# Giving every product of an attention and MLP kernel more than 64 rows of the array

## The chip, the cores and the metric

The kernel runs on one core of a Trainium2 chip. The metric is device time in microseconds, the median of several executions. The engines are TensorE (PE, whose weight loads are listed apart as PEld), VectorE (DVE), ScalarE (ACT) and GpSimd (POOL); the queue of SyncE (SP) issues every DMA. They run beside each other and wait for each other by semaphores; each works through its own list strictly in the order in which it was written.

## The reference

Four sequences of 576 positions pass through three blocks, in float32:

```python
# attention, per batch (4) and head (8), head_dim 64; cum is a running sum of max(s, 0)
scores = where(causal, -1e9, q @ k.T / 8 + minimum(-(cum[:, None] - cum[None, :]), 0))
x = softmax(scores) @ v                      # heads side by side: 576 x 512 per batch
# MLP: tokens, then channels
u = x + (relu(x.T @ w_tok1) @ w_tok2).T      # 576 -> 256 -> 576
y = u + relu(u @ w_ch1) @ w_ch2              # 512 -> 1536 -> 512
# gated output
gate = sigmoid(causal 5-tap convolution of y with conv_w)
out = (gate * (y @ w_val)) @ w_out
```

## The kernel before

Most products are done in float16 with each operand split into an upper and a lower half ("hi" and "lo"), so one float32 product becomes three: hi x hi, hi x lo and lo x hi, added up in PSUM.

**Stages.** A pair is two heads of one batch; there are 16 pairs. The queries of a head are cut into five tiles, `QT`: the first 64 positions, then four tiles of 128. Per pair the kernel loads q, k and v, scales them by a power of two found from their largest magnitude (`scales`, which asks `over_partitions` for a maximum across partitions: a transpose by PE, then a product with 3 rows), splits them, and turns q and k by a transposing DMA (`turn_qk`). Per tile `score` computes the scores, `expo` the exponentials, `p_split` cuts these into halves and turns them by a transposing DMA into `pT`, and `av` multiplies them by v (`v16`) into the PSUM bank `xbank`. Then `norm`, `x_value`, `x_split` and `x_turn` produce the pair's columns of x, and `tok1` and `tok2` the token MLP. Batch 0 is done "wide": its probabilities stay float32 and are turned by PE (`p_turn`) rather than by DMA. When all four pairs of a batch are done, its channel MLP and gated output run (`ch1`, `ch2`, `val`, `outp`; tiles `c`, `v`, `o`), and the next batch's attention is interleaved with them. The weights are decoded, summed (`ws`), scaled (`wf`) and split while batch 0 is under way.

**Rows of the array.** A product uses as many rows of the array as it sums over. In `av` the keys of a tile are cut from position 0 into blocks of 128, so the last block of each tile has 64 keys:

```python
K = TAIL if m == i else P              # TAIL is 64, P is 128
for pl, vl in ((0, 0), (0, 1), (1, 0)):
    PE.matmul(o, lhsT=self.pT[i, hh][:K, pl * (i + 1) + m, 0:M], rhs=self.v16[:K, vl, hh, m, :], ...)
```

`tok1` sums over the five tiles of positions, of which the first has 64 rows; `x_turn` transposes the first tile with 64 rows; the product of `over_partitions` has 1 or 3 rows, that of a weight's `scale` 1, and the transposes of the convolution's taps 5.

**What sets the order.** `ORDER` (from line 79) is a written list of steps, each an engine's letter and a task's number (P is PE, A ACT, V DVE, G POOL, S SP). `Plan.run` (line 422) goes through it and lets that task do its next step on that engine. A planner beside it keeps an assumed time for each engine, from costs in `cost_pe`, `cost_dma` and the like. Those times decide one thing in the program: where PE is assumed to wait, `keep_warm` (line 302) fills part of the gap with warming products of a zero tile (`idle`), whose result nobody reads.

Of the kernel before, what the change touches and what calls it, by code (L numbers as in the profile page):

```python
# [8 lines left out]
F32 = mybir.dt.float32  # L9
# [10 lines left out]
TINY = 2.0 ** -90  # L20
# [28 lines left out]
    u16=2, hT=7, mA=3, mB=2,  # L49
# [30 lines left out]
S0 V0 S5 P6 A7 A7 V7 P7 V7 S136 S8 A9 P1 S137 V1 V1 S136 S10 P1 V1 V1 A1 A9 V1 G137 S188 G188 V9 A1 V1 S1 A11 A11 P9  # L80
V9 S16 S19 P17 S25 S138 A2 A2 V2 A139 S28 V11 P11 V11 V12 P12 V12 V12 A18 A139 A139 P139 V139 V139 A18 V18 P139 V139
G3 A13 A20 A20 V139 V139 A140 V20 V13 A14 A141 V140 P18 V14 A15 V141 S142 S30 S142 S187 V18 V15 P20 V20 P26 A27 A27
V27 A29 V21 A29 V29 P27 P29 V27 P21 V21 A143 P158 P168 V21 V22 V22 A23 G23 A31 A31 P146 V29 P144 V144 A145 S32 V168
A169 V146 A147 P175 P172 S187 P152 V152 A153 P150 V150 S189 A33 P156 P148 A148 P166 A151 V172 P173 V156 V173 V31 P31
P154 A33 V33 V166 V31 A190 A154 A190 P154 V158 A167 A154 A190 S39 P40 A41 A41 P33 V33 V34 V175 P34 V34 V34 P170 A159
A157 A170 P190 V190 P176 V176 A177 V35 V190 P154 A154 P149 P149 P160 A160 V41 P170 P190 V190 V190 P160 P155 A174 S42
S44 S46 V35 P41 P155 A160 P160 V190 V191 V194 V191 A192 V192 S193 P178 A160 P161 P161 V162 A41 G41 A170 P170 A178
P178 A36 G36 A170 V162 V162 A178 P178 V162 V163 A164 V164 P171 P171 V37 V37 G38 V38 G4 G4 P165 A178 P179 P179 V180
A47 S53 S238 A45 A43 A43 V43 A47 V47 V180 A45 V45 S193 P226 P207 V226 P201 V207 P197 V201 P195 P227 P217 P209 A165
A181 A182 V182 P183 A183 V217 A218 S240 P184 P223 V197 A198 V24 V195 A196 P199 V209 A202 S239 G239 A208 P184 V223  # L90
P224 V224 S238 A241 P45 A184 V184 P43 V43 P203 V203 A199 P200 P200 A241 V227 P219 P185 A241 P241 A225 A204 A210 V241
V45 S56 P47 A47 P185 V241 P205 A205 P241 V185 V186 P211 A211 V241 V186 P54 A57 V241 P205 A205 V219 P211 A57 S58 S60
S67 V241 P205 A211 P211 A205 P206 P206 G47 V48 A228 S291 V57 P57 A211 P212 V245 V57 A242 V242 A243 V243 S244 S244
A220 A55 P212 V213 P48 V48 P229 V186 V213 P221 A229 P229 A221 G4 A55 V48 P221 V213 V213 V214 A229 V55 A221 P229 G49
P221 V49 P216 A221 A61 P68 A69 P55 P222 P222 A229 P230 V50 A69 V55 V215 V50 A59 V215 V69 P230 V231 A61 P246 V246
S289 P258 P254 A59 A247 S290 P69 V231 S289 V258 A259 P252 V252 A253 P274 V274 A216 P248 P260 P277 V248 A249 P250
A232 V254 A255 G51 G51 G52 V277 V260 A250 P275 V275 P278 P256 G233 P270 G290 A261 P262 A256 V69 S70 A276 A292 V270
A271 V61 P268 V278 P256 V268 A256 V59 S463 G463 P251 P251 A292 P256 A256 A292 A269 P61 V61 S72 A262 P59 V59 S74 P292
V292 P257 P272 A272 P262 A262 P272 V52 V292 P292 P262 A71 A272 A71 P257 V62 P62 A279 V292 V292 P272 V233 P235 P235
V292 A294 V71 V296 V294 P280 P71 A293 V293 S295 A235 V235 V62 V71 S76 A280 V62 P234 S295 A262 P263 P263 A73 A73 V73  # L100
V264 V264 V264 A272 A63 V63 P280 A75 A75 S462 P73 V73 S78 V64 A280 A234 S462 P236 P236 V236 V75 V264 P280 A280 P75
A77 A77 V265 P267 P273 A266 A267 V237 A75 S80 G75 V64 P305 P299 V77 P309 P325 A65 V266 P297 V297 A298 G65 G66 P77
A77 P273 V305 A306 V237 P321 V299 A300 A79 A79 V321 P319 V319 P281 P328 A320 V309 A310 V237 V325 P303 A465 A465 P311
# [12 lines left out]
S110 S112 A111 S114 V527 A97 V97 G98 V98 S501 A111 A523 V111 P111 P351 A348 V348 A346 V346 S577 G527 G99 A113 A113
P351 P353 P353 V99 A374 V523 S525 V111 A115 V375 A115 A350 V350 A352 V352 P369 A376 P355 P355 G100 V115 P115 G577
V100 P357 V507 A354 V354 A101 V101 V102 S121 P122 V102 P357 A526 V113 P113 S525 P528 P359 P359 P369 V105 V341 V528
P361 P361 S576 A115 S124 G115 A356 V356 P530 A123 S576 V103 V103 V113 S126 V375 V492 A508 A510 G510 S510 A123 A360
A125 A358 A125 V360 P363 P363 V116 P116 V123 P123 A579 A104 A579 V125 P125 V116 P365 P365 V530 P535 A531 V104 A579  # L120
V116 V358 P370 P367 P367 S578 A362 V376 V535 P553 V362 P544 A117 V492 V492 V117 A529 A532 G532 A364 A123 S128 V492
V493 P502 S532 P502 A366 G123 V364 P579 V366 V544 G118 V118 A127 P537 V537 P560 P511 P511 P398 P398 P370 A494 A368
V368 P542 A533 G533 S533 P371 A536 A539 G539 S539 A119 P371 A129 V125 A545 A127 V119 A120 A129 V579 A538 V127 P127
V579 P579 A547 V494 V129 P129 V120 V542 P373 P373 A543 V579 P555 P377 P377 V372 P495 V127 V579 G547 V579 A580 A540
G540 V553 A554 P563 G557 A581 V512 V512 V513 P534 A514 P534 V555 A556 P378 P378 V560 P561 A495 P380 P380 V580 S547
A583 V581 V557 V129 V130 P130 V561 P381 P381 V584 S540 P541 P541 V130 A546 V546 V514 P515 P516 A562 V130 S582 V379
V563 P564 V564 P516 S557 A566 V566 A558 A515 S582 P592 P587 V587 P585 P400 A516 A565 P594 V594 S546 P548 P548 P382
# [148 lines left out]
class Plan:  # L276
# [40 lines left out]
    def cost_pe(self, name, a, k):  # L317
        if name == "transpose":
            ns = max(cols(a[1]), a[1].shape[0]) / 2.4 * 2
        else:  # L320
            n = cols(k["rhs"])
            ns = max(40.0, n / 2.4 + 2.5) if k["rhs"].dtype != F32 else max(n, cols(k["lhsT"])) / 2.4 * 4
# [1359 lines left out]
```

## Time and profile before

| | |
|---|---|
| median of 3 runs | 734.91 us (733.26 to 738.43) |
| profiled execution | 735.01 us, of which the span of the instructions is 733.0 us |
| mean granted clock of TensorE | 0.974 of full speed |
| busy time | PE 695.4 us, DVE 517.3, ACT 397.9, POOL 178.6 |

Busy time is the time in which at least one instruction of the engine runs. A matmul's record also holds the time that it spends in the array after the next one has started, so PE can look busy while its products follow each other at a longer distance than they need to. What a product costs in a full queue is read from starts: the time from one group's first start to the next group's.

### The profile page before, as it was taken

The numbers are of one execution on the slowest core, as the hardware profiler recorded it, in microseconds if no ns is written. First come the engines' busy times: TensorE is split into PE (matmuls) and PEld (weight loads), VectorE is DVE, ScalarE is ACT, GpSimd is POOL, SyncE is SP. The second block draws the span as 40 slices with busy tenths as digits, with TensorE's granted clock in tenths as the row PEclk, the third lists the DMA queues.
The fourth block names the chain that finished last, engine by engine and source line by source line (L and its number), as shares of the span: only waits on it lengthen the run. The fifth ranks groups of instructions, "written<-read, shape, count | busy, mean of one in ns | idle before, by whom it ended". The sixth has DMA issues, their size and how long they took to land.

```text
span 733.0 us, 16461 instructions
## 1 busy us (share of the span) xinstructions
PE 695.4 (95%) x6340; PEld 522.4 (71%) x6340; DVE 517.3 (71%) x1508; ACT 397.9 (54%) x834; POOL 178.6 (24%) x264
## 2 busy tenths in 40 slices
PE   3899999998999999999999899999999999999997
PEld 3677877766677777676777677676777777668864
DVE  5777797658997887777688786598478852344663
ACT  4687787747775775545544563456556512213233
POOL 0112304122224334251232032332222312000410
PEclk9999999869999999999999999999999999999999
DMA  8645564736739576754646446382927320000001
GB/s 242 161 147 155 145 186 148 173 83 151 185 68 167 80 140 132 113 102 89 127 94 105 102 97 106 52 168 42 176 43 124 87 37 1 30 1 9 1 30 64
DMA packets 197911, 76.35 MB, mean 104 GB/s; under 512 B 188389, under 2 KB 188485, under 8 KB 197834
## 3 DMA queue, kind: packets, MB, share of 16 engines
q1 hardware_dynamic: 197834, 75.32, 48.0%
q8 instruction: 49, 0.80, 0.5%
q14 instruction: 28, 0.23, 0.1%
HBM read 33.50 MB, written 4.83 MB: 52 GB/s over the span
## 4 chain that ended last, share of the span: by engine, by line
PE 46%; DMA 5%; DVE 2%; SPq 2%; ACT 1%; POOL 1%; issue 1%; ACTq 0%; POOLq 0%; DVEq 0%
PE c L258 24%; PE o L258 6%; PE v L258 5%; PE xbank L258 4%; PE t L258 3%; DMA qkT<-qk 3%; PE S L258 3%; SPq L258 2%; DMA qk<-qkT 1%; PE xm L258 1%; DMA pT<-p 1%; PE xT L258 1%; DVE x L258 1%; ACT qk L258 0%; DMA stg<-in_k_dram 0%
## 5 line engine op out<-in xcount | busy, mean ns | idle before, releaser
L258 PEld LDWEIGHTS <-arena 128*128 128x128 f16 (+1 forms) x3168 | 287.1, 99 | 81.8 <-issue 6.5
L258 PE MATMUL c<-hT,arena 128*128 128x256 f16 (+1 forms) x1152 | 162.0, 288 | 0.0
L258 PE MATMUL c<-u,arena 128*128 128x256 f16 (+1 forms) x1152 | 159.9, 288 | 0.2 <-DVE hT L258 0.2
L258 ACT ACTIVATE x<-x,st 128x576 f32<-128x576 f32 (+4 forms) x160 | 86.7, 556 | 70.8 <-DVE st L258 69.8
L258 DVE CUSTOM_DVE_ANT_0 x<-S,mask,sc 64x64 f32<-64x64 f32 (+4 forms) x160 | 74.7, 482 | 44.6 <-PE S L258 41.0
L258 POOL TENSOR_TENSOR p<-x,p 64x64 f16<-64x64 f32 (+4 forms) x71 | 58.4, 824 | 155.6 <-ACT p L258 71.1
L258 PE MATMUL xbank<-v,pT 128*128 128x65 f16 (+3 forms) x1240 | 86.1, 209 | 1.5 <-DMA pT<-p 1.0
L258 ACT ACTIVATE hT<-c 128x320 f16<-128x320 f32 (+1 forms) x96 | 37.2, 403 | 87.7 <-PE c L258 87.7
L258 PE MATMUL S<-qk 67*64 67x64 f16 (+4 forms) x192 | 53.7, 290 | 12.2 <-DMA qk<-qkT 12.1
L258 DVE SCALAR_TENSOR_TENSOR hT<-c,hT 128x320 f16<-128x320 f32 (+1 forms) x96 | 41.2, 448 | 30.1 <-ACT hT L258 30.0
L258 DVE SCALAR_TENSOR_TENSOR gate<-R,cwt,gate 128x320 f32<-128x320 f32 (+1 forms) x116 | 60.5, 534 | 1.0
L258 PEld LDWEIGHTS <-pT 128*128 128x128 f16 (+2 forms) x1080 | 48.2, 98 | 14.9 <-issue 2.9
L258 PE MATMUL o<-arena,g 128*128 128x512 f16 (+1 forms) x240 | 57.2, 380 | 0.0
L258 PE MATMUL S<-qkT 128*64 128x64 f16 (+4 forms) x192 | 54.2, 293 | 0.0
L258 PE MATMUL v<-x,arena 128*128 128x256 f16 (+1 forms) x384 | 53.6, 286 | 0.0
L522 PE MATMUL xbank<-idle 128*128 128x112 f16 x573 | 47.1, 235 | 2.6 <-DVE x L258 1.9
L522 PEld LDWEIGHTS <-idle 128*128 128x128 f16 x573 | 38.6, 111 | 6.5 <-issue 3.2
L258 ACT ACTIVATE p<-x 128x576 f16<-128x576 f32 (+4 forms) x69 | 31.9, 464 | 16.6 <-DMA pT<-p 10.4
L258 PEld LDWEIGHTS <-g 128*128 128x128 f16 (+1 forms) x240 | 22.7, 100 | 23.5 <-issue 2.1
L258 PE MATMUL t<-xn,arena 128*128 128x128 f16 (+1 forms) x480 | 36.3, 225 | 0.4 <-ACT R L258 0.2
L258 ACT ACTIVATE gate<-gate 128x1280 f32<-128x1280 f32 (+1 forms) x24 | 27.9, 1162 | 14.7 <-DVE gate L258 14.4
L258 DVE TENSOR_TENSOR p<-x,p 128x448 f16<-128x448 f32 (+4 forms) x49 | 26.8, 551 | 7.8 <-ACT p L258 6.5
(212 smaller groups left out, 1021.1 us busy)
## 6 DMA issues: line engine op xcount, KB each, us to landing
raw<-in_moe_w_ch_dram SPq DMA_DIRECT2D x24, 512.0 KB
stg<-in_q_dram SPq DMA_DIRECT2D x16, 288.0 KB
stg<-in_k_dram SPq DMA_DIRECT2D x16, 288.0 KB
qk<-qkT SPq DMA_DIRECT2D x32, 144.0 KB
out_dram<-ot SPq DMA_DIRECT2D x16, 256.0 KB
vst<-in_v_dram SPq DMA_DIRECT2D x24, 128.0 KB
raw<-in_moe_w_val_dram SPq DMA_DIRECT2D x4, 512.0 KB
raw<-in_moe_w_out_dram SPq DMA_DIRECT2D x4, 512.0 KB
```

Source lines behind the costliest of these rows:

```text
L258: return f(*a, **k)
L522: plan.idle = lambda: nc.tensor.matmul(xbank[:, 400:512], lhsT=idle16, rhs=idle16[:, 0:112], start=True, stop=True)
```

## The change

Four kinds of products get more rows, and the order is a new list.

- `av`: the upper halves stand in the second half of the buffer `p16`, the lower halves in the first half, in groups of 64 keys that run backwards. Turned in blocks of 128, the middle block holds the first 64 keys twice, as lower and upper half; the upper halves follow in rising order and the lower halves in falling order, with the two groups of a block swapped. v is loaded so that its first 64 rows stand twice, and a copy of `v16` with the two halves of the partitions swapped (`vsw`, two DMAs for each of the 12 pairs that aren't wide) meets the swapped lower halves. A tile takes 3i+2 products a head instead of 3i+3, and its transposing DMA 2i+1 blocks instead of 2i+2.
- `tok1` and `x_turn`: `x32`, `xn` and the first piece of `w_tok1` have zero rows below row 64, and all 128 rows are used. `x_split` works on the first three tiles in one instruction.
- `over_partitions` and `scale`: the small vector `g` has 128 rows that are zero outside (four fixed buffers, `xg`).
- Wide `av`: `pg` has 128 rows, the lower ones zero.

The convolution's four transposes of taps share a bank and one ACT copy. Of the planner's costs, 184 ns are added where a product of at most 64 rows begins a step, and those of DMAs are changed.

```diff
@@ cost_pe, cost_dma
+        ns += 184.0 * (rows <= 64 and not self.held)
...
-            ns, wait, move = max(1200.0, 75.0 * blocks), 1300.0, 67.0 * blocks
+            ns, wait, move, after = max(1200.0, 165.0 * blocks - 260.0), 1000.0, 100.0 * blocks, 900.0 + 50.0 * blocks
@@ over_partitions
-        PE.matmul(ps[:, 256:256 + n], lhsT=g[:n].to_broadcast([n, P]), rhs=unit[:n, :n], start=True, stop=True)
+        PE.matmul(ps[:, 256:256 + n], lhsT=g.to_broadcast([P, P]), rhs=unit[:, :n], start=True, stop=True)
@@ Pair.load_v
-            else:
+            if not self.wide:
+                yield SY, "vst"
+                self.vst = vst
+                for j in range(2):
+                    SY.dma_start(vst[j * D:(j + 1) * D, :, 0, :], v[b, h0:h0 + 2, 0:D].rearrange("h p d -> p h d"))
+                for j in range(2):
+                    SY.dma_start(vst[:, j, 1:NK, :], v[b, h0 + j, D:S].rearrange("(n p) d -> p n d", p=P))
+                return
@@ Pair.split_v
+            yield SY, "vsw"
+            self.vsw = w = ap.tile([P, 2, NK - 1, DV], F16, tag="vsw", name=f"vsw_{self.nm}", bufs=BUFS["vsw"])
+            SY.dma_start(w[0:D], self.v16[D:, 0, :, 1:, :])
+            SY.dma_start(w[D:], self.v16[0:D, 0, :, 1:, :])
@@ Pair.p_split
-            pv = p16[:M, 0:2 * W1].rearrange("p (t c) -> p t c", t=2)[:, :, :N]
-            scaled(pv[:, 0], x[:M, :N], 1.0)
+            hi = p16[:M, N:2 * N]
+            lo = p16[:M, 0:N].rearrange("p (u c) -> p u c", c=D)[:, ::-1, :]
+            scaled(hi, x[:M, :N], 1.0)
...
-            SY.dma_start_transpose(out=pT[:, 0:2 * (i + 1), 0:M], in_=p16[:M, 0:2 * W1])
+            SY.dma_start_transpose(out=pT[:, 0:U, 0:M], in_=p16[:M, 0:2 * N])
@@ Pair.av
-                    K = TAIL if m == i else P
...
+                    terms = [(i + m, self.v16[:, vl, hh, m, :]) for vl in range(2)]
+                    if m:
+                        terms.append((i - m, self.vsw[:, hh, m - 1, :]))
+                    for blk, rhs in terms:
+                        PE.matmul(o, lhsT=self.pT[i, hh][:, blk, 0:M], rhs=rhs, start=(n == 0), stop=(n == 3 * i + 1))
@@ Pair.x_turn
-                PE.transpose(ps[:, q0 - b0:q0 - b0 + M], self.x32[:M, i, :], ident[:M, :M])
+                PE.transpose(ps[:, q0 - b0:q0 - b0 + P], x32[:, i, :], ident)
@@ Pair.tok1
-                            tv[:, tt, :], lhsT=wgt("t1", wl, kt, tt * P, P)[:K], rhs=self.xn[:K, xl, kt, :],
+                            tv[:, tt, :], lhsT=wgt("t1", wl, kt, tt * P, P), rhs=xn[:, xl, kt, :],
@@ ORDER (one line of 169)
-S0 V0 S5 P6 A7 A7 V7 P7 V7 S136 S8 A9 P1 S137 V1 V1 S136 S10 P1 V1 V1 A1 A9 V1 G137 S188 G188 V9 A1 V1 S1 A11 A11 P9
+...
```

The order of PE at one place, the transposes of pair 1_2 (batch 1, third pair; `xT` is the bank that `x_turn` writes). Before they follow a head's last products of `av`, and the first of them has 64 rows:

```order
L258 LDWEIGHTS pT_13_3_3783
L258 MATMUL xbank_81<-v16_1_2_3229,pT_13_3_3783 128x65
L258 MATMUL xT_1_2_0_3955<-ident_84,x32_1_2_3922 128x64
L258 MATMUL xT_1_2_0_3955<-ident_84,x32_1_2_3922 128x128 x2
L258 LDWEIGHTS arena_109
L258 MATMUL c1_0_1_10_3964<-u16_0_1_2691,arena_109 128x256
```

In the changed kernel three of 128 columns stand there in a row, between a product of the channel MLP and `av`:

```order
L258 LDWEIGHTS arena_117
L258 MATMUL c1_0_1_9_3957<-u16_0_1_2697,arena_117 128x256
L258 MATMUL xT_1_2_0_3976<-ident_92,x32_130 128x128 x3
L258 LDWEIGHTS pT_12_3_3782
L258 MATMUL xbank_81<-v16_1_2_3219,pT_12_3_3782 128x65
```

What moved is which tile's `av` stands next to the transposes, by a few products; the neighbourhood is the same.

The order of SP at the start of pair 2_0 (`qkT` its turned q and k, `qk2` the copies that its scores need; `pT` the probabilities of the pair ahead of it). Before:

```order
L258 DMA_TRANSPOSE qkT_2_0_4322<-qk16_2_0_4143 128x18x128
L258 DMA_TRANSPOSE pT_15_3_4332<-p16_0_119 128x8x128
L258 DMA_TRANSPOSE pT_14_3_4347<-p16_2_121 128x8x128
L258 DMA qk2_2_0_4016<-qkT_2_0_4322 64x1152 x2
L258 DMA_TRANSPOSE pT_15_4_4444<-p16_1_120 128x10x128
L258 DMA vst_2_1_4493<-in_v_dram 128x4x64 x2
```

Now:

```order
L258 DMA_TRANSPOSE pT_15_3_4311<-p16_15_3_4281 128x7x128
L258 DMA_TRANSPOSE qkT_2_0_4433<-qk16_2_0_4170 128x18x128
L258 DMA_TRANSPOSE pT_14_3_4453<-p16_14_3_4333 128x7x128
L258 DMA vsw_2_0_4479<-v16_2_0_4309 64x2x260 x2
L258 DMA qk2_2_0_4003<-qkT_2_0_4433 64x1152 x2
L258 DMA_TRANSPOSE pT_15_4_4484<-p16_15_4_4340 128x9x128
```

One transposing DMA has moved ahead of `qkT`, and the two copies `vsw` stand between `qkT` and `qk2`.

## Rows read from the trace of the kernel before

**Rows 1.** The page: busy time, share of span, instructions; the clock in 40 slices.

```profile
PE 695.4 (95%) x6340; PEld 522.4 (71%) x6340; DVE 517.3 (71%) x1508; ACT 397.9 (54%) x834; POOL 178.6 (24%) x264
...
PEclk9999999869999999999999999999999999999999
```

**Rows 2.** Windows: stretch, its us, busy us (instructions) of five engines, clock, DMA.

```profile
0.00:178.00 178.00, 153.25 (x1447) 123.02 (x1448) 129.67 (x404) 125.47 (x276) 35.67 (x56) 0.91 0.60 158
178.00:280.00 102.00, 101.30 (x969) 75.60 (x967) 89.03 (x256) 71.67 (x155) 36.86 (x50) 1.00 0.66 129
...
600.00:733.00 133.00, 129.06 (x969) 94.01 (x967) 61.22 (x146) 36.32 (x59) 16.95 (x24) 1.00 0.05 19
```

**Rows 3.** Waits of PE in 178 to 733: total us, times, longest.

```profile
PE S L258 <- DMA qk<-qkT: 7.3, 6, 2.9
```

**Rows 4.** Products by shape: rows*columns of the array, moving operand, count; busy us, mean ns.

```profile
L258 PE MATMUL xbank<-v,pT 64*128 64x65 f16 x288 | 25.2, 195 | 0.0
...
L258 PE MATMUL t<-xn,arena 64*128 64x128 f16 x96 | 11.1, 224 | 0.4 <-ACT R L258 0.2 <-DVE st L258 0.2
...
L258 PE MATMUL xm<-unit,xg 3*128 3x3 f32 x32 | 6.2, 263 | 0.0
...
L258 PE MATMUL xbank<-v,pT 64*64 64x65 f16 x72 | 4.8, 200 | 0.0
...
L258 PE MATMUL xT<-ident,x 64*128 64x64 f32 x16 | 4.3, 266 | 0.0
```

**Rows 5.** Timeline of PE, 344.5 to 349.5: start us, us, what, count.

```profile
345.16 1.79 PE L258 MATMUL c<-u,arena 128*128 128x320 f16 x12
346.89 0.37 PE L258 MATMUL xbank<-v,pT 64*64 64x65 f16 x6
347.19 1.80 PE L258 MATMUL c<-u,arena 128*128 128x320 f16 x12
348.83 0.27 PE L258 MATMUL xm<-ident,am 128*3 128x128 f32 x1
```

**Rows 6.** Timeline of PE, 410.9 to 414.

```profile
411.10 1.48 PE L258 MATMUL c<-u,arena 128*128 128x256 f16 x12
412.42 1.40 PE L258 MATMUL xbank<-v,pT 128*128 128x65 f16 x30
413.75 0.22 PE L258 MATMUL S<-qkT 128*64 128x64 f16 x1
```

**Rows 7.** Timeline of PE, 588 to 595.

```profile
588.60 1.22 PE L258 MATMUL xbank<-v,pT 128*128 128x65 f16 x24
589.74 1.48 PE L258 MATMUL c<-u,arena 128*128 128x256 f16 x12
591.16 0.64 PE L258 MATMUL xT<-ident,x 64*128 64x64 f32 x3
```

**Rows 8.** Windows behind two waits of PE.

```profile
406.70:410.10 3.40, 3.40 (x23) 2.49 (x21) 2.53 (x11) 1.03 (x4) 0.82 (x2) 0.51 0.97 207
...
444.30:447.70 3.40, 3.40 (x18) 2.38 (x17) 3.33 (x12) 1.81 (x8) 1.49 (x3) 0.50 1.21 199
```

**Rows 9.** Timeline of PE, 401 to 410.8: the wait ahead of the first window.

```profile
406.14 0.19 PE L258 MATMUL S<-qk 67*64 67x64 f16 x1 [2.85 <-DMA qk<-qkT]
```

**Rows 10.** Timeline of SP, 477 to 495: issue times.

```profile
478.03 2.69 SPq L258 DMA_TRANSPOSE qkT<-qk  x1
482.60 1.12 SPq L258 DMA_DIRECT2D qk<-qkT  x2
...
489.26 3.12 SPq L258 DMA_DIRECT2D vst<-in_v_dram  x3
```

**Rows 11.** The chain that ended last: start us, us, what.

```profile
403.57 2.53 DMA qk<-qkT
```

**Rows 12.** Windows of the first 178 us.

```profile
140.00:161.00 21.00, 21.00 (x118) 15.62 (x118) 10.12 (x34) 9.69 (x22) 2.40 (x3) 0.51 0.50 119
```

**Rows 13.** Products by shape: the warming products.

```profile
L522 PE MATMUL xbank<-idle 128*128 128x112 f16 x573 | 47.1, 235 | 2.6 <-DVE x L258 1.9 <-ACT x L258 0.4 <-DVE sums L258 0.3
```

More of the change, by code (lines that the diff above doesn't have):

```diff
@@ L48 @@
     B=7, X=1, stg=1, vst=1, qk16=1, qkT=2, qk2=2, v16=2, x=4, p16=3, pT=4, x32=1, xn=1, h1=1, pg=3,
-    u16=2, hT=7, mA=3, mB=2,
+    u16=2, hT=7, mA=3, mB=2, xg=4, vsw=2,
 )
@@ L318, in cost_pe @@
         if name == "transpose":
-            ns = max(cols(a[1]), a[1].shape[0]) / 2.4 * 2
-        else:
-            n = cols(k["rhs"])
-            ns = max(40.0, n / 2.4 + 2.5) if k["rhs"].dtype != F32 else max(n, cols(k["lhsT"])) / 2.4 * 4
+            rows = a[1].shape[0]
+            ns = max(cols(a[1]), rows) / 2.4 * 2
+        else:
+            n, rows = cols(k["rhs"]), k["lhsT"].shape[0]
+            ns = max(31.0, n / 2.4 + 2.5) if k["rhs"].dtype != F32 else max(n, cols(k["lhsT"])) / 2.4 * 4
+        ns += 184.0 * (rows <= 64 and not self.held)
         tick = int((self.now + self.held) // self.TICK)
@@ L351, in cost_dma @@
             run = out.shape[-1] * 4
-            ns, wait = 475.0, 1125.0
+            ns, wait, after = 590.0 if run <= 512 else 400.0, 1125.0, 900.0
             move = out.shape[0] * cols(out) * (2 if out.dtype == F16 else 4) / 360e3 * 1e3 * (2 if run < 512 else 1)
@@ L355, in cost_dma @@
         self.dma_free = max(t + wait, self.dma_free) + move
-        self.until = max(self.until, self.dma_free + 900)
+        self.until = max(self.until, self.dma_free + after)
         return ns
@@ L533, in over_partitions @@
         PE.transpose(ps[:n, 0:rows], src, ident[:rows, :rows])
-        yield V
-        g = const.tile([8, 1], F32, tag="xg", name="xg", bufs=3)
+        yield V, "xg"
+        g = free_xg.pop(0)
         V.tensor_reduce(g[:n], ps[:n, 0:rows], AX.X, ALU.max)
@@ L542, in over_partitions @@
         yield PE
-        PE.matmul(ps[:, 256:256 + n], lhsT=g[:n].to_broadcast([n, P]), rhs=unit[:n, :n], start=True, stop=True)
+        PE.matmul(ps[:, 256:256 + n], lhsT=g.to_broadcast([P, P]), rhs=unit[:, :n], start=True, stop=True)
+        free_xg.append(g)
+        give("xg")
         yield V
@@ L546, in over_partitions @@
         give("B")
+    free_xg = [const.tile([P, 1], F32, tag=f"xg{i}", name=f"xg{i}") for i in range(BUFS["xg"])]
+    for t in free_xg:
+        nc.vector.memset(t, 0.0)
     ident = const.tile([P, P], F32, tag="ident", name="ident")
@@ L765, in scale @@
             nm, pf = self.nm, pf_of(self.nm)
-            yield V
-            g = const.tile([1, 1], F32, tag="wsum", name=f"wsum_{nm}", bufs=2)
-            V.tensor_reduce(g, self.ps[0:1, :], AX.X, ALU.max)
-            V.tensor_scalar(g, g, TINY, W_MAX, ALU.max, ALU.min)
-            band(g)
+            yield V, "xg"
+            g = free_xg.pop(0)
+            V.tensor_reduce(g[0:1], self.ps[0:1, :], AX.X, ALU.max)
+            V.tensor_scalar(g[0:1], g[0:1], TINY, W_MAX, ALU.max, ALU.min)
+            band(g[0:1])
             give("B")
@@ L773, in scale @@
             ps = bank(f"wf_{nm}")
-            PE.matmul(ps[:, 0:1], lhsT=g.to_broadcast([1, P]), rhs=ident[0:1, 0:1], start=True, stop=True)
+            PE.matmul(ps[:, 0:1], lhsT=g.to_broadcast([P, P]), rhs=ident[:, 0:1], start=True, stop=True)
+            free_xg.append(g)
+            give("xg")
             yield V
@@ L811, in gated_block_kernel @@
     amR = [rp.tile([P, DT], F32, tag=f"amR{i}", name=f"amR{i}") for i in range(2)]
-    p16s = [ap.tile([P, 2 * SP], F16, tag=f"p16_{i}", name=f"p16_{i}") for i in range(BUFS["p16"])]
-    free16 = list(p16s)
+    pgs = [ap.tile([P, 2, P], F32, tag=f"pg_{i}", name=f"pg_{i}") for i in range(BUFS["pg"])]
+    x32 = ap.tile([P, NU, P], F32, tag="x32", name="x32")
+    xn = ap.tile([P, 2, NU, P], F16, tag="xn", name="xn")
+    vst = ap.tile([P, 2, NK, D], F32, tag="vst", name="vst")
+    free_pg = list(pgs)
     def init_state():
@@ L818, in init_state, with clear_rows @@
             G.memset(R[i][:, :, 0:HALO], 0.0)
-    def clear_p16():
-        for t in p16s:
+    def clear_rows():
+        for t in pgs:
             yield G
-            G.memset(t, 0.0)
+            G.memset(t[TAIL:], 0.0)
+        yield G
+        G.memset(x32[D:, 0, :], 0.0)
+        yield G
+        o, w, _ = Wt["t1"][0, 0]
+        G.memset(arena[D:, o:o + w], 0.0)
     class Pair:
@@ L858, in load_v @@
             G.memset(t[TAIL:, :, NK - 1, :], 0.0)
-            if self.wide:
-                G.memset(self.vst[:, :, :, D:DV], 1.0)
+            G.memset(self.vst[:, :, :, D:DV], 1.0)
         def load_ck(self):
@@ L1019, in p_turn @@
             yield A
-            self.pT[i, "pg"] = pg = ap.tile([TAIL, 2, P], F32, tag="pg", name=f"pg_{nm}", bufs=BUFS["pg"])
-            A.activation(pg[:, :, :M], p0[:, :, :M], AF.Copy)
+            self.pT[i, "pg"] = pg = free_pg.pop(0)
+            A.activation(pg[0:TAIL, :, :M], p0[:, :, :M], AF.Copy)
             give("B")
@@ L1029, in p_turn @@
                 yield A, "pT"
[L1030 removed]
+                pT = ap.tile([P, 2 * NK - 1, P], F16, tag="pT", name=f"pT_{nm}_{j}", bufs=BUFS["pT"])
                 self.pT[i, j] = pT.rearrange("p n c -> p (n c)").bitcast(F32)
@@ L1065, in av @@
                 give("v16")
+                if not self.wide:
+                    give("vsw")
         def spans(self, h):
@@ L1091, in x_value @@
             yield (ways, "x32") if h == 0 else ways
-            if h == 0:
-                self.x32 = ap.tile([P, NU, P], F32, tag="x32", name=f"x32_{self.nm}", bufs=BUFS["x32"])
             for M, i, n in self.spans(h):
@@ L1097, in x_value @@
                 rr = self.sums[:M, i:i + n, :].rearrange("p i h -> p (i h)")
-                out = self.x32[:M, i:i + n].rearrange("p i (h d) -> p (i h) d", h=2)
+                out = x32[:M, i:i + n].rearrange("p i (h d) -> p (i h) d", h=2)
                 if plan.engine is V:
@@ L1106, in x_split @@
         def x_split(self, h):
-            n = P * sum(x[2] for x in self.spans(h))
+            t = slice(0, 3) if h == 0 else slice(3, NU)
+            n = P * (t.stop - t.start)
             yield (one(n), "xn") if h == 0 else one(n)
-            if h == 0:
-                self.xn = ap.tile([P, 2, NU, P], F16, tag="xn", name=f"xn_{self.nm}", bufs=BUFS["xn"])
             kx = self.sc[:, 2:3]
-            for M, i, n in self.spans(h):
-                scaled(self.xn[:M, 0, i:i + n], self.x32[:M, i:i + n], kx[:M])
+            scaled(xn[:, 0, t], x32[:, t], kx)
             yield V
-            for M, i, n in self.spans(h):
-                rest(self.xn[:M, 1, i:i + n], self.x32[:M, i:i + n], kx[:M], self.xn[:M, 0, i:i + n])
+            rest(xn[:, 1, t], x32[:, t], kx, xn[:, 0, t])
         def x_turn(self, h):
@@ L1442, in gate_taps @@
         yield from decode(cst[:NKC], raw[:NKC, 0:DM, :], "mA")
+        yield PE, "B"
+        tp = bank("cwT")
         for d in range(DT):
-            yield PE, "B"
-            tp = bank(f"cwT{d}")
-            PE.transpose(tp[:, :NKC], cst[:NKC, d * P:(d + 1) * P], ident[:NKC, :NKC])
-            yield A
-            A.activation(cwt[:, d, :], tp[:, :NKC], AF.Copy)
-            give("B")
+            PE.transpose(tp[:, d * NKC:(d + 1) * NKC], cst[:NKC, d * P:(d + 1) * P], ident[:NKC, :NKC])
         give("mB")
+        yield A
+        A.activation(cwt.rearrange("p d t -> p (d t)"), tp[:, 0:DT * NKC], AF.Copy)
+        give("B")
     S0 = U0 + (NP * NU - 1) * PACE0 + LEAD0
@@ L1500, in plan_pair @@
                 for j in heads:
-                    step(t + o["prob"] + o["probj"] * j, "p_split", i, j, after=[("expo", i, j), t_p16] + before.get("pT", []))
+                    step(t + o["prob"] + o["probj"] * j, "p_split", i, j, after=[("expo", i, j)] + before.get("pT", []))
                 dep = [("p_split", i, 0), ("p_split", i, 1), ("split_v",)]
-            step(t + o["av"], "av", i, after=dep + ([("av", i - 1)] if i else []))
+            step(t + o["av"], "av", i, after=dep + ([("av", i - 1)] if i else [t_rows]))
             if i in (2, NU - 1):
```

360 lines of the change are left out of this document (177 added, 183 removed).

## The prediction

> **What bounds the kernel now.** I began with the page: PE is busy 95% of the span at nearly full clock, no other engine over 71% [rows 1]. A busy share averages over stages, so windows came next [rows 2]. They show three. From 0 to 178 us (batch 0's attention, the weights) no engine is near its limit: PE 153, DVE 130, ACT 125 of 178 us, the clock 0.91. From 178 to 600 us (three batches of attention between MLP work) PE is busy 101.3 of 102 us in the first window. From 600 us only MLP is left. Then the waits of PE after 178 us: the one that matters is the scores waiting for the copies of q and k, 7.3 us in six times, in 555 us [rows 3]. So after 178 us the time is PE's own list; a nanosecond taken out of that list is taken off the end, until something else is late.
>
> Busy is not the same as needed, so I looked at starts. Twelve products of 320 columns take 1.73 us from their first start to that of the next group when it has 64 rows (345.16 to 346.89), and 1.64 when it has 128 (347.19 to 348.83) [rows 5]: going from over 64 rows to at most 64 costs 0.09 us. Going back costs about as much: the six small products between them take 0.30 us [rows 5], of which six at 0.032 (below) explain 0.19. The same in `av`: thirty products take 1.33 us (412.42 to 413.75), twenty-four 1.14 (588.60 to 589.74) [rows 6, 7], so one costs 0.19/6 = 0.032 us; 24 x 0.032 = 0.77 leaves 0.37. In these groups each of two heads has three products of 64 rows at its end, so four crossings: 0.093 us each. As a control, the twelve products ahead of the thirty take 1.32 us, where `av` begins with 128 rows; the twelve ahead of the transposes, which begin with 64, take 1.42 [rows 6, 7].
>
> The Trainium skill, on the page "TensorE: Matmul & The Clock Gate", in the table of "Why this matters for your kernels", says that a lone product of 32 rows takes the time of one of 128, and its Part 2 that the row count doesn't matter; by that, crossings would be free and this change would have nothing to win from them. The trace agrees for the product and not for the change between the two kinds; the page "TensorEngine Tiling (Array Packing)", "Key Properties", does say that switching the tiling mode drains the engine.
>
> **The change, part by part.**
>
> *Crossings after 178 us.* 288 + 72 products of `av` have 64 rows, 360, or three for each of 10 tiles and heads of 12 pairs [rows 4]. Per pair, tiles 1 to 4 cross four times each, tile 0 twice (its heads stand together): 18, so 216; three tiles or so run before 178 us, leaving 206. `tok1`: 96 products [rows 4] are three for each of two halves of 16 pairs, 4 crossings a pair, 48 for the 12 pairs of batches 1 to 3. `x_turn`: 16 [rows 4], one a pair, 2 crossings, 24. The product with 3 rows (32 records [rows 4], two for each float32 product, 16 products) and its kind with 1 row: about 21 of them after 178 us, 42 crossings. Together 320. Some of the last stand beside each other, so I take 305, x 0.093 = **28.4 us**. The changed order has none of them left there. The first of the transposes gets 64 columns more, under 0.06 us x 12 = 0.7, which is taken off: 27.7.
>
> *Fewer products.* 3i+2 instead of 3i+3 over ten tiles and heads of 12 pairs is 120 fewer, x 0.032 = 3.8 us.
>
> *The front.* The same count gives some 130 crossings before 178 us (wide `av` 72, and `tok1`, `x_turn`, maxima, weights, taps), 12 us of PE's time. But PE has slack: 573 warming products fill 47.1 us there [rows 13]. It also runs at a granted clock of 0.51, the lower level of 1.2 GHz, from 140 to 161 us [rows 12], which costs 21 x 0.49 = 10 us of PE work. Upper bound: both come off the end, 22 us. Lower bound: by a count of the two orders there are 659 warming products ahead of the first product of `ch1` instead of 570; if none of the 89 meets a gap, at 47.1/573 = 0.082 us they add 7 us. I take a gain of 5: nearer to nothing than to 22, since PE's own list isn't what the front is made of.
>
> *SP.* Each of the 12 pairs gets two copies `vsw`, and four loads of v instead of three. Two copies cost SP 1.12 us, three loads up to 3.12 [rows 10], so 1.1 to 2.2 us a pair. A transposing DMA loses one block; I credit nothing. `vsw` waits for the split of v and stands ahead of `qk2` in SP's list, and the scores wait for `qk2`, where PE stood six times [rows 3]. Bounds: nothing, if SP is early, and 12 x 2.2 = 26 us if each pair is held by all of it. I take 4, six times 0.7, which is nearer to nothing, as PE stood nowhere else for SP.
>
> *The order.* The old costs give a transposing DMA of 18 blocks 1.35 us of SP, the new ones 2.71; the trace has 2.69 [rows 10]. So an order made with the new ones can place the scores later than the copies land. To gain: the 7.3 us and the window at half clock behind a wait of 2.85 us, 3.4 x 0.49 = 1.7, of which there are two [rows 8, 9]: 7.3 + 3.4 = 10.7. To lose: as much again, if other scores are late. I take a gain of 4, towards the middle of what the waits offer.
>
> *Off the path.* The reversed groups keep the size of each subtraction; `x_split` loses an instruction a pair; the one copy of the taps, the zero rows and the fixed buffers run on DVE, ACT or POOL, which have 13 us or more free in each window [rows 2]. If that cover goes, DVE is the first to tell: 89 of 102 us from 178 to 280.
>
> Sum, against the profiled execution (735.0, span 733.0; the median is 734.9, so nothing is shifted): 735 - 27.7 - 3.8 - 5 + 4 - 4 = 698.5. I predict **698 us**.
>
> **The rivals.**
>
> *More comes off* (677 to 686): the front at full clock and a steady stage without the waits for `qk2`, 735 - 27.7 - 3.8 - 12 - 9 = 682. For it: both losses stand in the trace. Against: the front is a chain of short dependent steps, and the half clock sits where float32 products and waits alternate, which they still do.
>
> *Half of it comes back as waits* (706 to 722): PE gives up 7 of the 102 us between 178 and 280, and DVE's 89 are then 94% of the 95 left; the SP list is longer. If half of the 31.5 us of the steady stage returns and the front gives nothing, 735 - 16 = 719. For it: DVE's 87% [rows 2]. Against: PE stood for DVE nowhere in that stage for as long as it did for `qk2` [rows 3].
>
> *Rows don't matter* (no change): what I read as crossings is some other fixed cost between groups, and the new groups pay it as well. Then 735 - 3.8 - 5 + 4 - 4 = 726. The rule of the Trainium skill above is this rival. Against: the two controls, where only the rows differ [rows 5 to 7].
>
> *Slower*: the scores wait for `qk2` behind `vsw` in each pair. A landing takes 2.5 us [rows 11]; if the split of v is late by that, PE stands 2.5 us in each of 12 pairs and runs the next window at half clock, as after the wait at 403 us [rows 8, 9]: 12 x (2.5 + 1.7) = 50 us, 735 - 31.5 + 50 = 753. It decides where the split of v ends over 4 us after `qkT` is issued. Against: that split depends on no more than the split of q and k does, and the DMA of `qkT` alone takes 2.69 us to issue.
>
> **How the numbers follow.** The forecast, 687 to 706, gets 0.66; more off 0.12; half back 0.14; rows don't matter 0.04; slower 0.04. Low 682 leaves out half of the second case, high 716 a third of the third and all of the last two: 0.06 + 0.05 + 0.08 = 0.19. One per cent, what a measurement can tell from no change, is 727.6 to 742.3. Faster takes the first three, 0.92; same 0.04, since 726 sits at its edge; slower 0.04.
>
> **What would show it.** In the trace after: no product of at most 64 rows after 178 us; a group of `av` for tiles 4 of two heads with 28 products taking 28 x 0.032 = 0.90 us instead of 1.33; twelve products ahead of the transposes at 1.32 instead of 1.42; the stretch from the first `ch1` to the end shorter by 28 to 36 us and the front by little. I am wrong if such groups still take over 1.1 us, if PE's waits after 178 us pass 20 us in total, or if the first `ch1` starts later than 178 us.

## The result and the profile after

The changed kernel takes 684.17 us (median of 4 runs, 682.67 to 687.78) against 736.28 for the kernel before (median of 4 runs): a ratio of 0.930, with a 95% interval from 0.925 to 0.9355. Timed a second time it gave 0.928 (0.925 to 0.9315). So it is faster by 52 us; 698 was forecast, with a range from 682 to 716.

The page of the changed kernel, the same two lines as [rows 1]; and two windows, cut where the first product of `ch1` starts (the columns are those of [rows 2]):

```profile
PE 640.7 (94%) x6335; PEld 496.9 (73%) x6335; DVE 516.0 (76%) x1469; ACT 397.9 (58%) x835; POOL 184.6 (27%) x277
...
PEclk9999999998899999999999999999999999999999
```

```profile
0.00:158.00 158.00, 131.71 (x1525) 110.72 (x1526) 133.51 (x398) 120.57 (x262) 41.10 (x63) 0.99 0.68 177
158.00:681.80 523.80, 509.00 (x4814) 386.22 (x4811) 382.46 (x1072) 277.28 (x574) 143.51 (x214) 1.00 0.45 89
```

The kernel before, cut in the same way:

```profile
0.00:176.60 176.60, 151.85 (x1441) 122.19 (x1442) 128.27 (x402) 124.07 (x274) 35.67 (x56) 0.92 0.61 159
176.60:733.00 556.40, 543.59 (x4902) 400.17 (x4899) 389.00 (x1107) 273.81 (x562) 142.88 (x208) 0.99 0.45 87
```

The stage from the first `ch1` on is 32.6 us shorter (556.4 to 523.8), with DVE and ACT as busy as they were. The front, the time up to the first `ch1`, is 18.6 us shorter, and its granted clock is 0.99 where it was 0.92. PE's busy time fell by 20.1 us in the front and by 34.6 in the rest; its idle time rose by 1.5 and 2.0.

In the list of products by shape four kinds of at most 64 rows are left, 17 records in all and all of them in the front, and the last blocks of `av` are among those of 128 rows (compare [rows 4]):

```profile
L258 PE MATMUL xbank<-vsw,pT 128*128 128x65 f16 x240 | 30.6, 195 | 0.0
...
L258 PE MATMUL t<-xn,arena 128*128 128x128 f16 x480 | 30.1, 219 | 0.0
...
L258 PE MATMUL xT<-ident,x 128*128 128x128 f32 x80 | 14.1, 276 | 0.0
...
L258 PE MATMUL p<-ident,x 64*64 64x64 f32 x8 | 1.4, 232 | 0.0
...
L258 PE MATMUL cwT<-ident,cst 5*128 5x5 f32 x4 | 0.4, 204 | 0.0
L258 PE MATMUL ws_t<-arena,ones 64*1 64x64 bf16 x4 | 0.4, 230 | 0.0
...
L258 PE MATMUL xm<-ident,cum 32*1 32x32 f32 x1 | 0.2, 205 | 4.8 <-DVE unit L574 4.8
```

What a tile of `av` costs now, in the timeline of PE (start, us, what, count). Tile 1, two heads:

```profile
320.92 1.79 PE L258 MATMUL c<-u,arena 128*128 128x320 f16 x12
322.55 0.29 PE L258 MATMUL xbank<-v,pT 128*128 128x65 f16 x4
322.67 0.19 PE L258 MATMUL xbank<-vsw,pT 128*128 128x65 f16 x1
322.70 0.29 PE L258 MATMUL xbank<-v,pT 128*128 128x65 f16 x4
322.82 0.20 PE L258 MATMUL xbank<-vsw,pT 128*128 128x65 f16 x1
322.86 1.79 PE L258 MATMUL c<-u,arena 128*128 128x320 f16 x12
```

Ten products follow each other in 0.31 us (322.55 to 322.86), 0.031 each, the price taken in the prediction, and the twelve ahead of them take 1.63: no crossing on either side. The 28 products of two tiles 4 take 0.85 us (348.64 to 349.49), where 0.90 was the sign to look for, and the twelve ahead of the transposes take 1.31 (518.25 to 519.56) instead of 1.42:

```profile
348.64 0.28 PE L258 MATMUL xbank<-v,pT 128*128 128x65 f16 x4
...
349.49 1.79 PE L258 MATMUL c<-hT,arena 128*128 128x320 f16 x12
```

PE's waits from the first `ch1` on (us in total, times, longest), which answer to [rows 3]:

```profile
PE S L258 <- DMA qk<-qkT: 5.6, 6, 1.7
PE xbank L258 <- DMA pT<-p: 2.5, 4, 0.8
PE S L258 <- DVE st L258: 0.7, 1, 0.7
PE v L258 <- DVE x L258: 0.7, 1, 0.7
```

The scores still wait for `qk2`, as often as before and for less time. No other wait has taken its place as the largest.

### The profile page after: what moved, and what is told of

Same layout as the page of the kernel before. It is cut to its first block, busy times and chain, and to the rows that moved or that the text cites. A ratio compares the mean times of both kernels' runs of the same rounds, so it can differ in the third digit from the quotient of the medians.

```text
span 681.8 us, 16448 instructions
## 1 busy us (share of the span) xinstructions
PE 640.7 (94%) x6335; PEld 496.9 (73%) x6335; DVE 516.0 (76%) x1469; ACT 397.9 (58%) x835; POOL 184.6 (27%) x277
## 4 chain that ended last, share of the span: by engine, by line
PE 55%; DVE 19%; DMA 8%; ACT 4%; SPq 4%; issue 4%; POOL 1%; DVEq 0%; ACTq 0%; POOLq 0%
PE c L258 26%; PE o L258 7%; PE xbank L258 5%; PE S L258 4%; PE v L258 4%; DMA qk<-qkT 4%; PE t L258 4%; DVE x L258 4%; SPq L258 4%; DMA pT<-p 3%; DVE arena L258 3%; DVE qk L258 2%; ACT x L258 2%; DVE gate L258 2%; PE xbank L525 1%
## 5 line engine op out<-in xcount | busy, mean ns | idle before, releaser
L258 PEld LDWEIGHTS <-arena 128*128 128x128 f16 x3168 | 287.3, 98 | 72.1 <-issue 3.4
L258 ACT ACTIVATE x<-x,st 64x64 f32<-64x64 f32 (+4 forms) x160 | 86.6, 556 | 72.2 <-DVE st L258 64.7
L258 POOL TENSOR_TENSOR p<-x,p 64x64 f16<-64x64 f32 (+4 forms) x82 | 67.5, 828 | 124.8 <-ACT p L258 81.7
L258 PE MATMUL xbank<-v,pT 128*128 128x65 f16 (+2 forms) x880 | 63.0, 209 | 3.2 <-DMA pT<-p 2.5
L258 PE MATMUL S<-qk 67*128 67x288 f16 (+4 forms) x192 | 51.6, 280 | 7.0 <-DMA qk<-qkT 6.5
L258 PE MATMUL S<-qkT 128*128 128x288 f16 (+4 forms) x192 | 52.3, 284 | 0.7 <-DVE st L258 0.7
L258 POOL TENSOR_SCALAR p<-x 128x576 f16<-128x576 f32 (+4 forms) x37 | 18.7, 505 | 107.5 <-ACT x L258 96.6
L258 PEld LDWEIGHTS <-pT 128*128 128x128 f16 (+1 forms) x960 | 37.9, 99 | 9.6 <-DMA pT<-p 4.7
L258 PEld LDWEIGHTS <-g 128*128 128x128 f16 (+1 forms) x240 | 23.0, 101 | 24.4 <-issue 3.3
L258 ACT ACTIVATE p<-x 128x192 f16<-128x192 f32 (+4 forms) x66 | 30.7, 468 | 15.6 <-DMA pT<-p 13.5
L258 DVE SCALAR_TENSOR_TENSOR R<-c,su,R 128x320 f32<-128x320 f32 (+1 forms) x32 | 16.0, 507 | 22.5 <-PE c L258 22.4
```

The costliest lines, as they stand in the source:

```text
L258: return f(*a, **k)
```

## The experiments

"Front" is the time to the first product of `ch1`, "rest" what follows, both of the profiled execution; "half" is the time in the front at a granted clock of 0.5; "warm" is the number of warming products in the front. These four are of one execution each, while the ratio is of several.

| kernel | ratio to before (interval) | front | half | warm | rest |
|---|---|---|---|---|---|
| before | 1 | 176.6 | 29.3 | 569 | 556.4 |
| over 64 rows, old order | 0.971 (0.968 to 0.975) | 174.3 | 44.4 | 569 | 539.7 |
| old rows, new order | 0.974 (0.970 to 0.977) | 171.3 | 23.9 | 621 | 546.4 |
| changed | 0.930 (0.925 to 0.9355) | 158.0 | 3.4 | 659 | 523.8 |
| changed, again | 0.928 (0.925 to 0.9315) | 157.9 | 3.4 | 659 | 524.6 |
| changed, old rows in the front | 0.9485 (0.9445 to 0.9525) | 170.3 | 20.5 | 619 | 527.1 |
| changed, no `vsw` | 0.926 (0.922 to 0.9305) | 161.6 | 13.7 | 658 | 522.1 |
| changed, no warming | 0.954 (0.950 to 0.958) | 166.2 | 31.0 | 0 | 528.0 |
| changed, more warming | 0.939 (0.935 to 0.942) | 160.3 | 3.4 | 853 | 529.2 |
| before, more warming | 0.990 (0.985 to 0.994) | 169.4 | 3.4 | 811 | 554.8 |
| over 64 rows, old order, more warming | 0.965 (0.9595 to 0.971) | 172.0 | 23.9 | 811 | 541.7 |
| changed, over 64 columns too | 0.922 (0.917 to 0.927) | 160.6 | 17.1 | 581 | 518.8 |
| the same, more warming | 0.923 (0.919 to 0.927) | 158.1 | 3.4 | 758 | 516.5 |

**The rows without the order.** The kernel before, in its own order, with zero rows or left-over probabilities filling the array.

```diff
-                    K = TAIL if m == i else P
+                    K = P
-        PE.matmul(ps[:, 256:256 + n], lhsT=g[:n].to_broadcast([n, P]), rhs=unit[:n, :n], start=True, stop=True)
+        PE.matmul(ps[:, 256:256 + n], lhsT=g.to_broadcast([P, P]), rhs=unit[:, :n], start=True, stop=True)
...
```

> The kernel before in its own order, with over 64 rows everywhere but in the sums and the 64x64 transposes of the weights' first piece and of batch 0: the last block of a tile in av takes 128 rows (the added rows hold left-over probabilities, so the output has terms that don't belong to it; the number of products stays), zero rows elsewhere. Theory 'crossings': the stage from the first product of ch1 to the end falls from 556 us by 304 x 0.093 = 28, whatever the order; the front by 0 to 12; total 695 to 708. Rival 'order' (the gain is that of the new list): 727 or more. Rival 'rows don't matter': 735.

The ratio is 0.971, 21 us; the rest fell by 16.7 us, the front by 2.3. "Rows don't matter" is out. But the 28 us did not all arrive: an old order on a faster PE waits more for `qk2`, 12.2 us in eight times instead of 7.3 in six, and the front spent 44 us at the lower clock, not 29:

```profile
PE S L258 <- DMA qk<-qkT: 12.2, 8, 3.5
```

The rest can be split. PE's busy time there fell from 543.6 to 515.3 us, by 28.3, which is what 304 crossings at 0.093 come to; its idle time rose by 11.6, from 12.8 to 24.4:

```profile
174.30:714.00 539.70, 515.29 (x4902) 391.67 (x4899) 391.26 (x1107) 273.24 (x561) 141.77 (x208) 0.99 0.43 89
```

**The order without the rows.** The changed kernel with at most 64 rows again wherever the kernel before had them. In `av` each head and tile leaves out the lower halves of the first 64 keys.

```diff
-                        PE.matmul(o, lhsT=self.pT[i, hh][:, blk, 0:M], rhs=rhs, start=(n == 0), stop=(n == 3 * i + 1))
+                        K = slice(0, P) if m else slice(D, P)
+                        PE.matmul(o, lhsT=self.pT[i, hh][K, blk, 0:M], rhs=rhs[K], start=(n == 0), stop=(n == 3 * i + 1))
...
```

> The changed kernel in its new order, with at most 64 rows again where they were: the first two products of each head and tile in av (these leave out the lower halves of the first 64 keys), tok1's first tile, the first transpose of x, the maxima, the weights' scales, wide av. Theory 'crossings': the stage from the first ch1 to the end rises from 524 us by 28, to 552; the front by up to 12; total 710 to 724. Rival 'order': within 4 us of 684.

The ratio is 0.974 (718.5 us) where the changed kernel's is 0.930: the old rows cost 32 us by the ratios. In the profiled executions they cost 22.6 us in the rest and 13.3 in the front. The 13.3 are not crossings alone: the front had 23.9 us at half clock instead of 3.4, and 38 warming products fewer, since the planner of this kernel charges 184 ns where a product of at most 64 rows begins a step and so sees smaller gaps. Its timeline shows the same ten products of a tile 1 with them:

```profile
343.82 0.40 PE L258 MATMUL xbank<-v,pT 64*128 64x65 f16 x4
344.06 0.19 PE L258 MATMUL xbank<-vsw,pT 128*128 128x65 f16 x1
344.19 0.40 PE L258 MATMUL xbank<-v,pT 64*128 64x65 f16 x4
344.42 0.20 PE L258 MATMUL xbank<-vsw,pT 128*128 128x65 f16 x1
344.46 1.79 PE L258 MATMUL c<-u,arena 128*128 128x320 f16 x12
```

They take 0.64 us (343.82 to 344.46) instead of 0.31: three crossings inside the group, 0.11 each, the fourth being ahead of it. Its rest counts 318 crossings in the trace. At 0.093 they are 29.6 us of PE; 22.6 came off the end. The difference is waits: the four listed for this kernel from its first `ch1` on add up to 4.3 us, those of the changed kernel to about 11. The windows say the same: without the crossings PE's busy time in the rest falls by 29.3 us (538.3 to 509.0), and its idle time rises by 6.7 (8.1 to 14.8).

```profile
PE S L258 <- ACT raw L258: 2.1, 1, 2.1
PE xbank L258 <- DMA pT<-p: 1.6, 2, 1.0
PE S L258 <- DMA qk<-qkT: 0.4, 1, 0.4
PE S L258 <- DVE st L258: 0.2, 1, 0.2
```

```profile
171.30:717.70 546.40, 538.29 (x4799) 388.48 (x4795) 382.61 (x1073) 278.69 (x574) 142.11 (x214) 1.00 0.42 86
```

**The crossings of the front alone.** Old rows in wide `av`, the weights' scales, and the wide pairs' `tok1` and `x_turn`; after the first `ch1` only one pair's edges change, four crossings.

```diff
-                        PE.matmul(o, lhsT=lhsT, rhs=self.vst[:, hh, m, :], start=(m == 0), stop=(m == i))
+                        K = TAIL if m == i else P
+                        PE.matmul(o, lhsT=lhsT[:K], rhs=self.vst[:K, hh, m, :], start=(m == 0), stop=(m == i))
...
```

> The changed kernel with at most 64 rows again in batch 0 and the weights' scales alone (wide av, tok1 and the first transpose of the wide pairs), some 100 crossings or 9 us of PE, all ahead of the first ch1, which now starts at 158 us. Theory A 'the front is PE's list too': the first ch1 8 to 12 us later, total 692 to 696. Theory B 'the front gained by its order and its clock' (half clock for 38 us before, 7 now): 0 to 3 us later, total 684 to 687.

The first `ch1` starts at 170.3 us, 12.3 later: past theory A's 8 to 12 and far from theory B's 0 to 3. But two other things moved with it: 20.5 us ran at half clock instead of 3.4, and the planner filled in 40 warming products fewer in the front (619 for 659). The three runs that the ratio rests on span 694.3 us at a mean clock of 0.987, 697.4 at 0.980 and 699.7 at 0.978, so part of the 12 goes with the clock, and this run does not isolate the crossings.

**The clock.** The kernel before with a larger share of its planned gaps filled, 835 warming products for 573:

```diff
-WARM_FROM, WARM_FILL, GAP1 = 12e3, 0.65, 13.87
+WARM_FROM, WARM_FILL, GAP1 = 12e3, 0.9, 13.87
```

> The kernel before with 835 warming products instead of 573, nothing else changed. Theory 'clock': its front runs 29 us at the lower level (0.5 granted), most of it from 140 to 161 us; if the added products keep it up, the first ch1 starts 8 to 14 us earlier than at 177 us and the total is 722 to 729. Rival 'filler is work': the clock is not what holds the front, and 262 products at 0.05 to 0.1 us stand in PE's list: 735 to 750.

The clock of the stretch of [rows 12] rose from 0.51 to 1.00, and the front became 7.2 us shorter, a little under what was expected; the ratio is 0.990, 729.1 us, at the upper edge of the 722 to 729 expected.

```profile
140.00:161.00 21.00, 20.86 (x232) 16.38 (x231) 16.45 (x58) 17.14 (x41) 7.32 (x13) 1.00 0.58 149
```

The other way round, the changed kernel with `WARM_FILL` 0:

> The changed kernel with no warming product at all (688 left out). Theory 'clock': the front falls to the lower level where PE waits, most of its 158 us, and the first ch1 starts at 175 us or later: total 700 or more. Rival 'filler is work': 48 us of PE's busy time are gone from the front, total 670 to 684.

The ratio is 0.954. The front grew by 8.2 us with 31 us at half clock, and not to the 175 us expected; that the filler's own time went too would explain it, but no run shows it. The total did pass 700 (701.3); the profiled execution was the shortest of its four (696.1), so 8.2 is probably on the low side. And the changed kernel with `WARM_FILL` 0.9, 936 warming products:

> The changed kernel with 936 warming products for 688. Its clock is at 0.995 already (7 us at the lower level): theory 'clock' gives it nothing to win, 682 to 687; theory 'filler is work' makes it slower by 248 x 0.05 = 12 us, 694 to 698.

It is slower, 692.5 us, between the ranges of the two theories. With the clock up already, filler is work: 2.3 us in the front. The 5.4 in the rest are more than the 54 warming products added there would take at 0.05 us; the scores' wait for `qk2` grew to 10.1 us.

```profile
PE S L258 <- DMA qk<-qkT: 10.1, 8, 2.5
```

**Are rows and clock additive in the front?** The first experiment with `WARM_FILL` 0.9:

> The kernel before in its own order, with over 64 rows as in the run without a new order, and 835 warming products for 573. Without them its front had 44 us at the lower level and the first ch1 at 174 us. Theory 'the front is crossings and clock together, additive': clock 7 us (as in the kernel before with more warming products), crossings 8: the first ch1 at 160 to 164 us, total 700 to 706. Rival 'the new order made the front': 170 us or later, total 712 to 718.

The first `ch1` came at 172.0 us and the total is 715.6, the rival's numbers. But the condition wasn't met: the front still had 23.9 us at half clock, 17 of them from 137 us on. So it doesn't tell the order from the clock. Its run with the highest mean clock, 0.988, took 706.6 us, next to the first theory's 700 to 706; that theory isn't out.

**SP.** The changed kernel without the 24 copies; the lower halves then meet halves of v that don't belong to them.

```diff
-                        terms.append((i - m, self.vsw[:, hh, m - 1, :]))
+                        terms.append((i - m, self.v16[:, 0, hh, m, :]))
...
-            SY.dma_start(w[0:D], self.v16[D:, 0, :, 1:, :])
-            SY.dma_start(w[D:], self.v16[0:D, 0, :, 1:, :])
```

> The changed kernel without the 24 copies vsw: the lower halves meet v in the unswapped order (so their terms are wrong). Theory 'SP holds the scores': after the first ch1 4 us less, the waits of scores for qk2 near nothing, total 680. Rival 'SP has room': within 1 us of the changed kernel, the waits as they are. Upper end of my prediction's bounds: 26 us less.

0.926, inside the changed kernel's interval; the rest is 1.7 us shorter, where two executions of the changed kernel differ by 0.8, and the scores' wait for `qk2` is much as it was (4.8 us in four times, 5.6 in six with the copies). SP has room for them. The fourth load of v was not tried by itself.

**A version that goes on.** The changed kernel's timeline shows the same price for columns. Twelve products of 256 columns take 1.31 us up to scores with 128 columns of weights and 1.41 up to scores with 64:

```profile
341.13 1.47 PE L258 MATMUL v<-x,arena 128*128 128x256 f16 x12
342.44 0.30 PE L258 MATMUL S<-qkT 128*128 128x320 f16 x1
...
343.88 1.47 PE L258 MATMUL v<-x,arena 128*128 128x256 f16 x12
345.29 0.22 PE L258 MATMUL S<-qkT 128*64 128x64 f16 x1
345.34 0.20 PE L258 MATMUL S<-qk 67*64 67x64 f16 x1
345.47 0.26 PE L258 MATMUL S<-qkT 128*128 128x192 f16 x1
```

So tile 0 was computed for 128 queries, the last output tile for 128 positions, and the weights' sums in 128 columns, with half or more of each unused.

```diff
@@ score, p_turn, av (and M = P after N in expo and p_split)
-            q0, M = QT[i]
+            q0, M = QT[i][0], P
@@ dec
-                        self.ps[0:1, :], lhsT=ones[:rows], rhs=x[:, f:f + self.nsum],
+                        self.ps, lhsT=ones[:rows].to_broadcast([rows, P]), rhs=x[:, f:f + self.nsum],
@@ outp
-                    ps[:M, :DM], lhsT=self.g16[:, gl, kt, o:o + M], rhs=wgt("wo", wl, kt, 0, DM),
+                    ps[:, :DM], lhsT=self.g16[:, gl, kt, o + M - P:o + M], rhs=wgt("wo", wl, kt, 0, DM),
...
```

> The changed kernel with over 64 columns of the array as well: tile 0 of each head is computed for 128 queries, of which 64 are used; the last tile of the output product takes 128 rows of x, of which 64 are used; the weights' sums are made in 128 columns, of which one is read. In the trace of the changed kernel a product of 320 columns takes 229 ns up to a float16 product with 64 columns of weights, and 136 otherwise. Theory 'crossings by columns cost as much': after the first ch1 about 95 float16 ones x 0.093 = 9 us less, the front 0 to 8 less: 667 to 676. Rival 'the wider loads of weights cost what the crossings did', or another limit is reached: 681 to 688.

0.922 (680.2 us): the rest fell by 5.0 us; the front did not. The planner had filled in 613 warming products for 688, and 17.1 us of the front ran at half clock. One more execution of the same kernel:

> A single look at the kernel with over 64 columns as well, for the spread of its clock: with a granted clock of 0.99 a span of 672 to 675, with 0.98 of 678 to 682.

The span was 673.4 us at a clock of 0.992, with a rest of 515.6: one kernel's rest differs by 3.2 us between two executions. With `WARM_FILL` 0.9, beside the changed kernel on one chip:

> The changed kernel with over 64 columns as well and 841 warming products for 613. Theory 'clock': the front's 10 to 17 us at the lower level go, the spread between runs closes, total 669 to 675, under the changed kernel by 10 or more. Rival 'filler is work': 678 to 684.

> The changed kernel once more, beside the ones below: 0.925 to 0.935 of the kernel before.

679.7 against 685.0 us, 0.923 (0.919 to 0.927) against 0.928 (0.925 to 0.9315). So the total that went with the clock, 669 to 675, did not come, and the spread between runs did not close: the spans still go from 674.6 us at a mean clock of 0.997 to 679.2 at 0.989. The total lies in the range of the rival, that filler is work. The rest of the profiled executions is 516.5 us against 524.6, 8.1 less where 9 were expected. The scores' tile 0 shows it: the twelve products take 1.31 us now.

```profile
343.49 1.47 PE L258 MATMUL v<-x,arena 128*128 128x256 f16 x12
344.80 0.19 PE L258 MATMUL S<-qkT 128*128 128x64 f16 x1
344.83 0.20 PE L258 MATMUL S<-qk 67*128 67x64 f16 x1
```

The two intervals of the totals just overlap, so half a per cent is likely and not proven. With either amount of filler, over 64 columns gives the lowest ratios of the kernels tried.

## Why the prediction was right, and where its sizes were off

**The mechanism and the rest.** 27.7 for crossings, 3.8 for fewer products, and SP and the order cancelling made 31.5 us; 32.6 were measured. That the two agree so closely is luck, for the sum hides two errors, of 5 and of 6 us, that cancel. Crossings were worth 22.6 us at the end, not 27.7, as the experiment with the old rows shows. Their count and price were right: PE's busy time in the rest shrank by 28.3 us with the old order and by 29.3 with the new one. But 11.6 and 6.7 us of that came back as idle time, where the prediction had none come back from a faster PE. The new order, the fewer products and the small changes that came with them were worth 10.0 (the rest of old rows in the new order against before), not 3.8 + 4 - 4 = 3.8. So rows and order do not simply add up: with the old order the rows gave 16.7 us, with the new one 22.6, and the scores' wait for `qk2` is where the old order lost most (12.2 us against 5.6).

**The front** is the step that was mis-sized. The prediction had both causes and put their bound at 22 us, and then took 5, "since PE's own list isn't what the front is made of". 18.6 were measured, so the sign "the front by little" failed, and all of it is PE's busy time (20.1 us less busy, 1.5 more idle). That reading came from 573 warming products, taken as slack. They are not slack in the sense of time to spare: without them the front is longer. The clock is shown to be one cause: 7.2 us in the kernel before, by filler alone. What is left shows where both kernels hold it. With 3.4 us at half clock each, the front is 169.4 us in the kernel before with more warming, and 158.0 in the changed kernel, or 160.3 with more warming as well: 9 to 11 us at the same clock. The traces count 139 crossings in the front before and 13 in the changed kernel; 126 at 0.093 are 11.7. So the size fits the crossings, and the upper bound of 22, both causes coming off the end, was nearly right. But the order differs between these fronts too, and the run that puts old rows back into the front (108 crossings, 10 us) moved the first `ch1` by 12.3 together with the clock and the filler, so the crossings' own share is not shown.

What stays open is why the changed kernel keeps its clock. The old rows in the new order lose it for 24 us, the new rows in the old order for 44, both together for 3.4. The amount of filler differs as well, 621, 569 and 659 warming products in these fronts, and is a rival to rows and order as the reason; it is not the whole reason, for 811 in the old order with the new rows still left 23.9 us at half clock.

**SP.** The 4 us taken for the copies were too many; their removal gives the rest 1.7. The upper bound of 26 was far off: SP's list is longer, but the scores wait 5.6 us with the copies and 4.8 without.

**The order.** The 4 us taken for scores placed better can't be separated from the rest; the wait itself went from 7.3 to 5.6 us.

**The rivals.** "Rows don't matter" fell with the first experiment. The Trainium skill (page "TensorE: Matmul & The Clock Gate", table of "Why this matters for your kernels") has a single product of 32 rows take the time of one of 128; the words of its Part 2 on the row count are about loading the weights. Here neighbouring products of `av` start 0.04 us apart with 64 rows and 0.03 with 128 (medians in the rest of the kernel before), so the rule nearly holds for one product of 64 rows, and not for a list that mixes the two. The Trainium skill also says that changing the tiling mode drains the engine ("TensorEngine Tiling (Array Packing)", "Key Properties"). The 0.09 to 0.11 us a crossing would fit that if a product of at most 64 rows counts as another mode, which no run here shows. "Half comes back as waits" was right in kind: about a quarter did with the new order, 6.7 of 29.3 us, and 11.6 of 28.3 with the old one. DVE was not the limit it was feared to be; the scores' DMAs were. "More comes off" came nearest in total, with 682; it looked for 9 of its extra 16 us in the rest, and nearly all of the extra gain came in the front.

## What to carry to other kernels

Read starts, not durations: two groups that differ only in what follows them give the price of a change of rows or columns, 0.09 us here, and a count of such changes gives what a PE-bound stage can win at most: of 28 to 29 us taken off PE's list, 17 came off the end with the old order and 23 with the new one. Such a gain and a new order belong together, for a faster PE meets waits that the old order had covered. Filler that holds the clock is neither free nor slack: with the clock lost, 262 more warming products made the front 7 us shorter here; with the clock held, 248 more cost the whole kernel 7 to 8.

## What the runs showed that was not expected

Columns cross at much the same price as rows for float16 products: 0.10 us from 128 to 64 columns of weights. Float32 transposes with 3 columns don't pay it: the twelve products ahead of one take 1.64 us [rows 5], as ahead of 128 columns. And the time of one kernel follows its clock from run to run: the kernel with over 64 columns spans 672.9 us at a mean clock of 0.992, 677.4 at 0.986, 679.4 at 0.982 and 681.8 at 0.977.
